# Multiplying the output gate into a copy of the last 128 W_down columns during chunk 3

## The chip, the cores and the metric

The kernel runs on one core of one Trainium2 chip. The metric is the device time in microseconds (us) of one execution. The rounds of the experiments ran on three chips (numbers 5, 3 and 1), each beside runs of the kernel before, and a ratio compares kernels of the same rounds alone. The profile's span is about 1.7 us shorter than the device time of the same run (829.4 against 831.17 us in the first profile), so spans are compared with spans and times with times.

## The reference

A transformer block with adaptive layer-norm: linear attention, then a SwiGLU feed-forward network. S = 2048 tokens, D = 1024, F = 3584, all bf16. Only the end matters for this change:

```
x = A_x
sa, ca, ga, sb, cb, gb = ...            # six rows of D values from the condition c
h = layernorm(x) * (1 + ca) + sa
x = x + ga * attention(h)
h = layernorm(x) * (1 + cb) + sb
x = x + gb * ((silu(h @ w_gate) * (h @ w_up)) @ w_down)
return x
```

`gb` holds one value per output column. Multiplying the product's column n by gb[n] is therefore the same as multiplying column n of `w_down` by gb[n] beforehand, up to rounding to bf16.

## The kernel before

The feed-forward part works in 4 chunks of 512 tokens. In each chunk the kernel first computes 28 tiles of gate and up products (8 + 8 matmuls of 128x512 each), which ScalarE and VectorE turn into the 28 tiles of `AT`. Then 4 token tiles of 128 rows are multiplied with W_down, which lies in SBUF (`WD_A`, `WD_B`) for all chunks. SBUF is the memory in which the kernel keeps its tiles; PSUM (`PS`, in banks) is the one into which its matmuls write. The last part of the program, with the code that the change touches:

```
for ch in range(NCH):                       # NCH = 4
    nxt = ch + 1 if ch + 1 < NCH else None  # None in chunk 3, the last
    for ft in range(NFT):                   # NFT = 28
        gbank, ubank = 2 - (ft % 2) * 2, 3 - (ft % 2) * 2      # PSUM banks alternate
        # ... 8 matmuls into gbank, 8 into ubank ...
        P.act("activation", out=SG[:, ft % 2, :], in_=PS[:, gbank, :], func=ACT.Silu)
        P.dve("tensor_tensor", out=AT[:, ft, :], in0=SG[:, ft % 2, :], in1=PS[:, ubank, :], op=ALU.mult)
        # ... loads; in chunk 0 the gate row GB_B is computed; next chunk's layer norm ...
    for j in range(4):                      # token tiles of the chunk
        st = 4 * ch + j
        bb = 4 + 2 * (st % 2)
        last = st == NST - 1
        # ... if not last: 28 x 2 matmuls into banks bb, bb + 1 ...
        for nh in range(2):                 # halves of the output row
            i = nh
            parts = [(0, 384, bb + 1), (384, 512, 4)] if last and nh == 1 else [(0, 512, bb + nh)]
            for (c0, c1, pb) in parts:
                if last:
                    # ... 28 matmuls over columns c0:c1 of this half ...
                xs = XRES[:, st, nh * 512 + c0:nh * 512 + c1]
                gbs = GB_B[:, nh * 512 + c0:nh * 512 + c1]
                if c0 > 0:
                    P.dve("tensor_tensor", out=UT[:, i, c0:c1], in0=PS[:, pb, c0:c1], in1=gbs, op=ALU.mult)
                else:
                    P.act("activation", out=ATT[:, i, c0:c1], in_=PS[:, pb, c0:c1], func=ACT.Copy)
                    P.dve("tensor_tensor", out=UT[:, i, c0:c1], in0=ATT[:, i, c0:c1], in1=gbs, op=ALU.mult)
                P.dve("tensor_tensor", out=xs, in0=xs, in1=UT[:, i, c0:c1], op=ALU.add)
                out_ops.append(P.dma("out", ov[:, st, nh * 512 + c0:nh * 512 + c1], xs))
```

A helper records every operation, finds from the memory it reads and writes which other engines it has to wait for, and sets the semaphores. In the profile every compute instruction therefore carries that helper's line (L176), and groups are told apart by their tiles.

## Time and profile before

| | before |
|---|---|
| time, median of the first 3 runs | 831.27 us (831.02 to 831.39) |
| span of the profiled run | 829.438 us |
| end of TensorE's last matmul | 826.91 us |
| tail: from there to the end of the span | 2.52 us |

Ends and tails, here and below, are taken from the trace in nanoseconds. The rows of the views print start and duration rounded, so that a sum of them can be off by 0.01 us.

The engines' busy time, the first part of the profile of the kernel before (us, share of the span, instructions):

```profile
PE 824.2 (99%) x4083; PEld 379.2 (46%) x4083; DVE 310.3 (37%) x665; ACT 196.3 (24%) x335; POOL 40.7 (5%) x58
```

The end of the chain of waits (before, from 822 us on; start, duration, what):

```profile
821.94 4.99 PE ps L176 x49
826.93 0.02 issue
826.95 0.30 DVE ut L176
827.25 0.02 issue
827.28 0.23 DVE xres L176
```

The timeline of the same end (before; start, duration, engine, instruction, count, idle time before it and who ended it):

```profile
826.08 0.83 PE L176 MATMUL ps<-wd_b,at 128*128 128x128 bf16 x12
826.38 0.36 DVE L176 TENSOR_TENSOR xres<-xres,ut 128x384 bf16<-128x384 bf16 x1
826.77 1.09 SPq L176 DMA_DIRECT2D out_dram<-xres  x2
826.95 0.29 DVE L176 TENSOR_TENSOR ut<-ps,gb_b 128x128 bf16<-128x128 f32 x1 [0.21 <-PE ps L176]
827.28 0.23 DVE L176 TENSOR_TENSOR xres<-xres,ut 128x128 bf16<-128x128 bf16 x1
```

The last two VectorE instructions are the pair that the change goes for: 0.29 and 0.23 us with a gap between them. The `SPq` row merges the issues of two outputs, of 96 and 32 KB, and its 1.09 us run from the start of the first issue to the end of the second (one issue takes 0.33 us).

VectorE in chunk 3, where the new work is to go (before, timeline of VectorE):

```profile
712.92 0.69 DVE L176 TENSOR_TENSOR at<-sg,ps 128x512 bf16<-128x512 bf16 x1 [2.77 <-PE ps L176]
716.38 0.69 DVE L176 TENSOR_TENSOR at<-sg,ps 128x512 bf16<-128x512 bf16 x1 [2.77 <-PE ps L176]
```

The number in brackets says that VectorE sat idle for 2.77 us of every 3.45 us and that TensorE ended the idle time.

The two last output DMAs (before, DMA view from 826 us on; KB, us from issue to landing):

```profile
out_dram<-xres SPq DMA_DIRECT2D x1, 96.0 KB, 1.6
out_dram<-xres SPq DMA_DIRECT2D x1, 32.0 KB, 1.5
```

### The profile page before, as it was taken

To read this page: it belongs to the slowest core of one execution; us is meant where nothing else is said; L and a number is where in the kernel's file an instruction comes from. 1 tells how busy PE (TensorE), PEld (TensorE's weight loads), DVE (VectorE), ACT (ScalarE), POOL (GpSimd) and SP (SyncE) were. 2 spreads that over 40 slices of the span, in tenths; PEclk is the share of its full clock that TensorE was granted. 3 is DMA by queue.
4 is the path that set the end of the run, shared out by engine and by line. 5 is a ranking of instruction groups with operands and counts; after the bars stand their busy time and mean duration, and the time that the engine had idled before them with its cause. 6 is when DMAs were issued, how large, how long until landed. Compare 5 with 4: busy or idle time off the path is not lost.

```text
span 829.4 us, 10016 instructions
## 1 busy us (share of the span) xinstructions
PE 824.2 (99%) x4083; PEld 379.2 (46%) x4083; DVE 310.3 (37%) x665; ACT 196.3 (24%) x335; POOL 40.7 (5%) x58
## 2 busy tenths in 40 slices
PE   8999999999999999999999999999999999999998
PEld 4544444444444444444444444444444444444444
DVE  5797986666955521111221111122111111111111
ACT  3757641323242111011111101111110111111011
POOL 1010000000130000030000003000000300000000
PEclk9999999999999999999999999999999999999999
DMA  9969655938397985700455571045557004553000
GB/s 324 283 151 230 151 158 172 191 113 304 59 258 226 290 255 154 194 25 13 125 151 152 153 188 31 14 125 153 153 150 193 26 17 123 153 152 89 0 26 26
DMA packets 199246, 119.29 MB, mean 144 GB/s; under 512 B 57880, under 2 KB 182944, under 8 KB 199200
## 3 DMA queue, kind: packets, MB, share of 16 engines
q1 hardware_dynamic: 199184, 118.65, 52.7%
q8 instruction: 32, 0.52, 0.3%
q14 instruction: 14, 0.11, 0.0%
q10 hardware_dynamic: 16, 0.00, 0.0%
HBM read 100.67 MB, written 4.33 MB: 127 GB/s over the span
## 4 chain that ended last, share of the span: by engine, by line
PE 96%; DMA 2%; DVE 1%; SPq 0%; ACT 0%; issue 0%; POOL 0%; ACTq 0%
PE ps L176 96%; DMA z_row<-zr 1%; DMA zb<-z_row 0%; DVE stats L176 0%; DMA xres<-in_A_x_dram 0%; DVE mhl L176 0%; SPq L176 0%; DVE xres L176 0%; DVE pqt L176 0%; POOL rstd L176 0%; DVE g L176 0%; DVE mv L176 0%; ACT gtmp L176 0%; ACT e L176 0%; DVE ve L176 0%
## 5 line engine op out<-in xcount | busy, mean ns | idle before, releaser
L176 PE MATMUL ps<-h2t,gug 128*128 128x512 bf16 x896 | 211.7, 379 | 0.0
L176 PE MATMUL ps<-h2t,guu 128*128 128x512 bf16 x896 | 211.7, 379 | 0.0
L176 DVE TENSOR_TENSOR at<-sg,ps 128x512 bf16<-128x512 bf16 x112 | 77.0, 687 | 284.8 <-PE ps L176 283.2
L176 ACT ACTIVATE sg<-ps 128x512 bf16<-128x512 f32 x112 | 66.9, 597 | 309.7 <-PE ps L176 309.7
L176 PEld LDWEIGHTS ps<-h2t,guu 128*128 128x128 bf16 x896 | 87.7, 98 | 105.7
L176 PEld LDWEIGHTS ps<-h2t,gug 128*128 128x128 bf16 x896 | 87.6, 98 | 105.5
L176 PE MATMUL ps<-wd_a,at 128*128 128x512 bf16 (+2 forms) x528 | 113.5, 373 | 0.0
L176 PE MATMUL ps<-ht,wqk 128*128 128x512 bf16 x512 | 111.8, 379 | 0.1
L176 PE MATMUL ps<-wd_b,at 128*128 128x512 bf16 (+2 forms) x396 | 85.8, 373 | 0.0
L176 PEld LDWEIGHTS ps<-wd_a,at 128*128 128x128 bf16 x528 | 51.1, 98 | 59.8
L176 DVE TENSOR_TENSOR ut<-att,gb_b 128x512 bf16<-128x512 bf16 (+1 forms) x32 | 13.5, 421 | 167.7 <-ACT att L176 167.7
L176 PEld LDWEIGHTS ps<-ht,wqk 128*128 128x128 bf16 x512 | 49.4, 98 | 58.7 <-DVE ht L176 0.4
L176 ACT ACTIVATE att<-ps 128x512 bf16<-128x512 f32 (+1 forms) x32 | 17.4, 591 | 182.1 <-PE ps L176 182.1
L176 PEld LDWEIGHTS ps<-wd_b,at 128*128 128x128 bf16 x396 | 38.3, 98 | 44.7
L176 PE MATMUL ps<-pk,xres 128*128 128x512 bf16 x256 | 56.7, 379 | 0.1
L176 PE MATMUL ps<-mw,pqt 128*128 128x512 bf16 x256 | 56.3, 379 | 0.0
L176 POOL TENSOR_SCALAR h2t<-h2t,modcol 128x512 bf16<-128x512 bf16 x32 | 26.4, 841 | 383.1 <-DMA h2t<-xn 383.1
L176 ACT ACTIVATE e<-ps 128x512 bf16<-128x512 f32 x56 | 33.1, 603 | 31.8 <-PE ps L176 19.6
L176 PEld LDWEIGHTS ps<-mw,pqt 128*128 128x128 bf16 x256 | 24.9, 98 | 30.2 <-DVE xres L176 0.4
L176 PEld LDWEIGHTS ps<-pk,xres 128*128 128x128 bf16 x256 | 24.8, 98 | 30.3 <-DVE g L176 0.6
L176 ACT ACTIVATE junk<-xres 128x1024 bf16<-128x1024 bf16 x24 | 25.4, 1058 | 35.1 <-DVE xres L176 34.9
L176 DVE SCALAR_TENSOR_TENSOR xres<-ps,xres 128x512 bf16<-128x512 f32 x32 | 21.4, 688 | 12.3 <-PE ps L176 11.5
(102 smaller groups left out, 341.1 us busy)
## 6 DMA issues: line engine op xcount, KB each, us to landing
gug<-in_B_w_gate_dram SPq DMA_DIRECT2D x56, 512.0 KB, 4.0
guu<-in_B_w_up_dram SPq DMA_DIRECT2D x56, 512.0 KB, 5.3
xres<-in_A_x_dram SPq DMA_DIRECT2D x20, 256.0 KB, 7.7
rb<-recip_den SPq DMA_DIRECT2D x8, 512.0 KB, 12.1
stgx<-in_w_mod_dram SPq DMA_DIRECT2D x2, 2048.0 KB, 7.9
wd_a<-in_B_w_down_dram SPq DMA_DIRECT2D x4, 1024.0 KB, 7.4
out_dram<-xres SPq DMA_DIRECT2D x31, 128.0 KB, 1.7
xres<-in_A_x_dram SPq DMA_DIRECT2D x3, 1024.0 KB, 14.2
```

The costliest lines, as they stand in the source:

```text
L176: return getattr(e, method)(**kw)
```

## The change

The intent: take one VectorE instruction out of the tail. In chunk 3 VectorE has idle time, so there it multiplies the last 128 columns of W_down by their gate into a separate copy (a copy, because 7 KB per partition are free and the other token tiles keep using the ungated weights). The last 28 matmuls read the copy. What comes out of PSUM is then already gated, and one add of the residual finishes it.

```diff
+        WDG = T("wdg", 144 * KB, [128, NFT, 128], BF16)
...
+                if nxt is None and ft in (8, 12):
+                    f0, f1 = (0, 16) if ft == 8 else (16, NFT)
+                    wt = WD_A if ft == 8 else WD_B
+                    P.dve("tensor_tensor", out=WDG[:, f0:f1, :], in0=wt[:, :, 896:1024],
+                          in1=GB_B[:, 896:1024].unsqueeze(1).to_broadcast([128, f1 - f0, 128]), op=ALU.mult)
...
-                                     rhs=WD(ft)[:, nh * 512 + c0:nh * 512 + c1], start=(ft == 0), stop=(ft == NFT - 1))
+                                     rhs=WDG[:, ft, :] if c0 > 0 else WD(ft)[:, nh * 512 + c0:nh * 512 + c1],
+                                     start=(ft == 0), stop=(ft == NFT - 1))
...
                         if c0 > 0:
-                            P.dve("tensor_tensor", out=UT[:, i, c0:c1], in0=PS[:, pb, c0:c1], in1=gbs, op=ALU.mult)
+                            P.dve("tensor_tensor", out=xs, in0=PS[:, pb, c0:c1], in1=xs, op=ALU.add)
                         else:
                             P.act("activation", out=ATT[:, i, c0:c1], in_=PS[:, pb, c0:c1], func=ACT.Copy)
                             P.dve("tensor_tensor", out=UT[:, i, c0:c1], in0=ATT[:, i, c0:c1], in1=gbs, op=ALU.mult)
-                        P.dve("tensor_tensor", out=xs, in0=xs, in1=UT[:, i, c0:c1], op=ALU.add)
+                            P.dve("tensor_tensor", out=xs, in0=xs, in1=UT[:, i, c0:c1], op=ALU.add)
```

## The prediction

> **What bounds the kernel now.** TensorE. The page's first part has PE busy 824.2 us of a span of 829.4 (99%), DVE 37%; the granted clock is full in every slice. The chain of waits is 96% PE. So only two things move the time: stalls of PE, and the tail after its last matmul.
>
> The tail, from the timeline: the last matmul ends at 826.91. DVE `ut<-ps,gb_b` (128x128, PSUM source) starts at 826.95 and takes 0.29; `xres<-xres,ut` starts at 827.28 and takes 0.23 (end 827.51); the last output DMA (32 KB) is issued at 827.53; it lands about 1.5 us later (DMA view), and the span ends at 829.44. So 2.53 us of tail, 0.56 of it the two VectorE instructions with their gap.
>
> **What the change removes.** The pair becomes one add that reads PSUM and xres, with the shape and operand kinds of the present `ut<-ps,gb_b`: 0.29 us, from 826.95 to 827.24. Removed from the critical path: 0.23 plus the gap of 0.03 to 0.04, so 0.27 us.
>
> **What it adds.** Two VectorE multiplies in chunk 3 (2048 and 1536 elements per partition). An all-SBUF bf16 tensor_tensor took 1.215 us at 2048 elements (`pqt<-pqt,rb`) and 0.42 at 512 (`ut<-att,gb_b`); by their slope the estimates are 1.22 and 0.95 us. [...] Both fit: in chunk 3 DVE idles 2.77 us between consecutive 0.69 us `at<-sg,ps` instructions, and their banks alternate, which gives further slack. Off the critical path: 0 us. PE does the same 28 matmuls of 128 columns; only the moving operand's address differs. The copy lies in space that holds nothing live then, and PE already waits for later VectorE work (the last AT tile), so no new wait. GpSimd has nothing to do in chunk 3.
>
> **What may eat the gain.** The last DMA is issued 0.27 us earlier, at about 827.26, while the preceding 96 KB output (issued 826.77, for 0.33) is moving. In the DMA view its packets run from about 827.57 to 828.06 and the last one's from about 828.27 to 828.57. Moved 0.27 earlier they would start at about 828.00: overlap of 0.06 us at most. I expect 0.2 to 0.27 us to survive. [...] the trace agrees that the time is mostly not data movement (0.3 us of 1.5), and the change does not touch it.
>
> **Prediction.** 831.27 - 0.26 = 831.0 us, range 830.6 to 831.4 (the three runs of before spread 0.37 us, more than the effect). Faster by over 2%: 0.003; within 2%: 0.994; slower by over 2%: 0.003.
>
> **What would show it.** Right: after PE's last matmul one DVE instruction of about 0.29 us, the last output issue about 0.35 us after PE's end instead of 0.62, landing about 1.5 us later; two new DVE instructions of 1.2 and 0.95 us in chunk 3 with PE's idle unchanged; tail about 2.25 us. Wrong: a longer add; a landing of 1.7 us or more (gain lost to contention with the 96 KB transfer); a PE gap behind the multiplies; multiplies over 3.5 us.
>
> **What would make it wrong.** A strided, broadcast multiply far slower than estimated and stalling PE, or landings at the end that hide the gain. Neither reaches 2%.

For the multiplies' 1.22 and 0.95 us the slope between the two measured instructions stays as the ground; that the stride and the broadcast would cost nothing was the assumption, not shown before the run. The 0.3 us of 1.5 is what the trace of before gives for the last output's data packets.

## The result, and the profile after

| | before | after |
|---|---|---|
| time, median of 6 runs each | 831.26 us (831.02 to 832.30) | 831.10 us (830.85 to 831.27) |
| span of the profiled run | 829.438 us | 829.344 us |
| end of TensorE's last matmul | 826.91 us | 827.07 us |
| tail | 2.52 us | 2.27 us |

The ratio of after to before is 0.9997, 95% interval 0.9984 to 1.001: the same. A ratio is the mean time of one kernel's fast runs over that of the other's of the same rounds, so it is not quite the ratio of the medians.

The end of the chain of waits (after, from 822 us on):

```profile
821.94 5.15 PE ps L176 x50
827.09 0.02 issue
827.11 0.29 DVE xres L176
```

The timeline of the end (after):

```profile
825.35 1.73 PE L176 MATMUL ps<-wdg,at 128*128 128x128 bf16 x28
...
826.54 0.36 DVE L176 TENSOR_TENSOR xres<-xres,ut 128x384 bf16<-128x384 bf16 x1
826.93 0.83 SPq L176 DMA_DIRECT2D out_dram<-xres  x2
827.11 0.29 DVE L176 TENSOR_TENSOR xres<-ps,xres 128x128 bf16<-128x128 f32 x1 [0.21 <-PE ps L176]
```

The pair has become one instruction of 0.29 us. The two issues now end 0.83 us after the first one starts instead of 1.09 us: the last output leaves 0.26 us sooner after the one before it.

The two multiplies in chunk 3 (after, timeline of VectorE):

```profile
713.08 0.69 DVE L176 TENSOR_TENSOR at<-sg,ps 128x512 bf16<-128x512 bf16 x1 [2.77 <-PE ps L176]
713.69 1.22 DVE L176 TENSOR_TENSOR wdg<-wd_a,gb_b 128x2048 bf16<-128x2048 bf16 x1
716.54 0.69 DVE L176 TENSOR_TENSOR at<-sg,ps 128x512 bf16<-128x512 bf16 x1 [1.63 <-PE ps L176]
...
727.50 0.95 DVE L176 TENSOR_TENSOR wdg<-wd_b,gb_b 128x1536 bf16<-128x1536 bf16 x1
730.35 0.69 DVE L176 TENSOR_TENSOR at<-sg,ps 128x512 bf16<-128x512 bf16 x1 [1.90 <-PE ps L176]
```

They only eat into the idle time in front of the next `AT` tile: 2.77 us became 1.63 and 1.90. The `AT` tiles themselves keep their pace.

The last two outputs (after, DMA view from 826 us on):

```profile
out_dram<-xres SPq DMA_DIRECT2D x1, 96.0 KB, 1.7
out_dram<-xres SPq DMA_DIRECT2D x1, 32.0 KB, 1.5
```

So the tail is 0.25 us shorter: the last output is issued 0.36 us after TensorE's end instead of 0.62, and lands as long after its issue as before (1.49 against 1.48 us). But TensorE ended 0.16 us later in this trace, and the span shows only the difference, 0.09 us. Does the change delay TensorE? I matched the VectorE instructions of the two traces one by one, in order, and looked at how their start times differ. The difference jumps to 0.41 us at 7.85 us, in the loads and transposes of the start, wanders until 168 us, and from there on its settled value is 0.16 us right up to the end (short excursions of VectorE epilogues come back to it). It is 0.16 us just before the first multiply at 713 us and 0.16 us just after. So nothing is lost where the change is; whether that holds in general is a question for the experiments.

### The profile page after: what moved, and what is told of

Its sections match the earlier page's. It is cut to its first block, busy times and chain, and to the rows that moved or that the text cites. A ratio compares the mean times of both kernels' runs of the same rounds, so it can differ in the third digit from the quotient of the medians.

```text
span 829.3 us, 10017 instructions
## 1 busy us (share of the span) xinstructions
PE 823.3 (99%) x4083; PEld 378.8 (46%) x4083; DVE 312.9 (38%) x666; ACT 196.3 (24%) x335; POOL 40.5 (5%) x58
## 4 chain that ended last, share of the span: by engine, by line
PE 98%; DMA 1%; DVE 0%; ACT 0%; SPq 0%; POOL 0%; issue 0%
PE ps L176 98%; DMA xres<-in_A_x_dram 1%; ACT ht L176 0%; DVE xres L176 0%; SPq L176 0%; POOL rstd L176 0%; DVE stats L176 0%; DVE mv L176 0%; DVE ve L176 0%
## 5 line engine op out<-in xcount | busy, mean ns | idle before, releaser
L176 PE MATMUL ps<-wd_a,at 128*128 128x512 bf16 (+1 forms) x512 | 112.4, 377 | 0.0
L176 PE MATMUL ps<-wd_b,at 128*128 128x512 bf16 (+1 forms) x384 | 85.0, 377 | 0.0
```

The costliest lines, as they stand in the source:

```text
L176: return getattr(e, method)(**kw)
```

## The experiments

Twelve experiments were run. The theory, T: the change takes the quarter of a microsecond out of the tail and does nothing else. The rivals: R1, the gated copy costs TensorE time; R2, the end of the span isn't set by the chain "VectorE, last output"; R3, the slack for VectorE work in chunk 3 is only the idle time that the timeline shows; R4, the last output contends with the 96 KB one before it.

Each experiment left one trace. Its two numbers, TensorE's end and the tail, say more than its times:

| kernel | time, median (lowest to highest) | TensorE's end | tail |
|---|---|---|---|
| before | 831.26 (831.02 to 832.30) | 826.91 | 2.52 |
| before_again | 831.49 (831.35 to 831.66) | 827.23 | 2.52 |
| copy_only | 831.24 (830.85 to 831.50) | 827.23 | 2.53 |
| after | 831.10 (830.85 to 831.27) | 827.07 | 2.27 |
| after_again | 831.34 (830.58 to 831.88) | 827.68 | 2.27 |
| add_only | 830.94 (830.68 to 831.09) | 826.83 | 2.27 |
| mult_x5 | 831.03 (830.92 to 831.19) | 826.96 | 2.28 |
| fold_all | 830.93 (830.78 to 832.08) | 826.93 | 2.26 |
| one_dma | 831.09 (831.02 to 831.46) | 826.83 | 2.50 |
| fold_256 | 831.43 (830.91 to 832.82) | 828.58 | 2.50 |
| tail_x9 | 833.94 (833.76 to 833.99) | 827.05 | 5.12 |
| mult_x8 | 835.57 (833.55 to 836.41) | 829.55 | 2.26 |
| mult_x8_again | 835.55 (one run, state unknown) | 831.57 | 2.26 |
| mult_x10 | 838.49 (838.01 to 839.98) | 835.98 | 2.27 |

### after_again: the changed kernel, unaltered

Expected:

> The changed kernel again, unaltered. Theory T (only the tail after TensorE's last matmul changed): tail from TensorE's end to the span's end about 2.22 us against 2.51 before, time 0.1 to 0.4 us below before. Rival R1 (the gated copy costs TensorE time, so TensorE ends later): the last matmul ends later than in before by 0.1 us or more in this trace too, with the delay entering after 713 us, where the first multiply runs. If instead the delay enters in the first 10 us and has another sign or size than the 0.16 us of the first trace, it is start-up jitter.

Measured: median 831.34 us, ratio 1.0 (0.9987 to 1.0012). The time that T expected was missed: this time the changed kernel wasn't faster at all. The tail was 2.27 us again, 0.26 us shorter than before; the figures in the text above, 2.22 and 2.51, were both a little low. TensorE ended 0.77 us later than in the trace of before, and matching the instructions shows the delay coming in between 7 and 42 us; its settled value is 0.77 us at 168 us and still 0.77 us at 658 us and after. The start-up gives each run another offset, here three times the size of the gain. R1's late entry of a delay isn't there.

### copy_only: the multiplies without their use

```diff
# to the kernel before: the two multiplies into WDG as in the change; nothing reads WDG
```

Expected:

> The two multiplies alone: the gated copy is written and never read, the epilogue is that of before. T: same time as before within 0.15 us, tail 2.51 us as before, multiplies of 1.22 and 0.95 us, TensorE undisturbed after 713 us. R1: slower than before by 0.1 to 0.2 us, and TensorE's offset against before grows after 713 us.

Measured: 831.24 us against 831.26 us, ratio 0.9998 (0.9985 to 1.001). The tail was 2.53 us and the multiplies took 1.218 and 0.952 us. The offset against before was 0.32 us at 168 us and 0.32 us at the end. The copy costs TensorE nothing: R1 falls.

### add_only: the short epilogue without the copy

```diff
# to the changed kernel: no WDG, no multiplies; the last 28 matmuls read the ungated W_down
-                                     rhs=WDG[:, ft, :] if c0 > 0 else WD(ft)[...],
+                                     rhs=WD(ft)[:, nh * 512 + c0:nh * 512 + c1],
```

The last 128 columns are ungated, so the result is wrong on purpose.

Expected:

> The one-add epilogue alone: no copy, the last 128 columns stay ungated, so the result is wrong there on purpose. T: same as the changed kernel, 0.1 to 0.4 us below before, tail about 2.22 us. R1: faster than the changed kernel by 0.1 us or more, because the copy's cost is gone.

Measured: 830.94 us against 831.26 us, ratio 0.9995 (0.9981 to 1.0009), tail 2.27 us. The whole gain is in the epilogue, and it is there without the copy, at the same size. Its time is 0.16 to 0.4 us below that of the changed kernel, which R1 would have liked, but its TensorE simply ended early (826.83 us) by an offset that its trace again brings in at the start (settled at -0.08 us by 168 us and to the end), and copy_only had already shown the copy to be free.

### tail_x9: a longer tail on purpose

```diff
# to the kernel before, the multiply of the last 128 columns out of PSUM
-                            P.dve("tensor_tensor", out=UT[:, i, c0:c1], in0=PS[:, pb, c0:c1], in1=gbs, op=ALU.mult)
+                            for _ in range(9):
+                                P.dve("tensor_tensor", out=UT[:, i, c0:c1], in0=PS[:, pb, c0:c1], in1=gbs, op=ALU.mult)
```

Expected:

> Before, with the last 128-column multiply out of PSUM done nine times instead of once (same result). T: each repetition adds its own time to the span one for one: 8 x (0.29 plus a gap of 0.00 to 0.04) = 2.3 to 2.6 us slower than before, clear of the noise, no change before TensorE's end. Rival R2 (the end of the span is set by something else than the chain VectorE, last DMA, for instance the 96 KB output or a fixed end of program): less than 2 us slower.

Measured: 833.94 us against 831.26 us, ratio 1.0031 (1.0017 to 1.0045). The timeline of its end:

```profile
827.09 2.89 DVE L176 TENSOR_TENSOR ut<-ps,gb_b 128x128 bf16<-128x128 f32 x9 [0.21 <-PE ps L176]
830.01 0.22 DVE L176 TENSOR_TENSOR xres<-xres,ut 128x128 bf16<-128x128 bf16 x1
```

Nine took 2.89 us where one took 0.29, so eight more cost 2.60 us; the tail grew by as much (5.12 against 2.52). The medians differ by 2.68 us, and the rest is within the scatter of the runs. (The traced run's mean clock of 0.998 comes from a fall to half at 829.13 us, when TensorE had no work left, so it cost nothing.) VectorE's time behind the last matmul counts one for one: R2 falls. This is the only kernel of the tail whose effect is clear of the noise in the times themselves.

### before_again: the kernel before against itself

Expected:

> The kernel before, submitted against itself: the noise of this comparison. Both theories: ratio 1.000; tail about 2.53 us in the trace; TensorE's end anywhere between 826.8 and 827.7 us, as in the six traces so far, with the shift entering in the first 45 us. If all traces of the unchanged kernel end TensorE before 827.0 us, a systematic cost of the change in the start-up phase stays possible.

Measured: 831.49 us, against 831.17 us for the runs of the same kernel beside it, ratio 1.0002 (0.9989 to 1.0015). The five runs lie between 831.35 and 831.66 us; eight of the nine beside them between 830.92 and 831.27, one at 832.60. Two medians of one and the same program thus differ by 0.32 us, more than the gain that is looked for. In its trace TensorE ended at 827.23 us, with a settled offset of 0.32 us from 168 us to the end and the tail at 2.52 us. A late TensorE is no sign of the change.

### mult_x5 and mult_x8: how much room VectorE has in chunk 3

```diff
# to the changed kernel, n = 5 or 8
+                    for _ in range(n if ft == 8 else 1):
                         P.dve("tensor_tensor", out=WDG[:, f0:f1, :], in0=wt[:, :, 896:1024], ...
```

Expected of the first:

> The changed kernel with the first multiply written five times in a row (same result): 6.1 us of VectorE work instead of 1.22, more than the 2.77 us of idle up to the next AT tile. T (slack also holds the alternate bank): AT tile 9 ends 6.8 us after AT tile 8, the up matmuls that reuse its bank start 7.9 us after it (estimate: 2.77 plus three groups of 1.73), so TensorE does not wait and the time is that of the changed kernel. Rival R3 (slack is only the 2.77 us of idle): 3.3 us slower.

Measured: 831.03 us, ratio 0.9997 (0.9983 to 1.001), tail 2.27 us. The five multiplies ran from 713.57 us for 6.26 us in a row, `AT` tile 9 was late by about 3.3 us, and TensorE didn't wait at all. R3 falls: with the alternate PSUM bank, 6.26 us of work fitted where the timeline shows 2.77 us of idle time.

Expected of the second:

> The same eight times: 9.75 us of VectorE work. T: AT tile 9 ends 10.4 us after AT tile 8, 2.6 us after its bank is wanted: TensorE waits 2.5 to 2.7 us once, ended by VectorE, and the kernel is 2.5 to 2.7 us slower than the changed kernel. R3: 7 us slower. If there is no wait at all, the slack was underestimated.

Measured: 835.57 us, ratio 1.0054 (1.0039 to 1.007). Its profiled run, of 833.55 us, shows the wait as T expected it, 2.7 us, ended by VectorE (mult_x8, timeline):

```profile
713.29 10.03 DVE L176 TENSOR_TENSOR wdg<-wd_a,gb_b 128x2048 bf16<-128x2048 bf16 x8
...
723.24 1.28 DVE L176 TENSOR_TENSOR at<-sg,ps 128x512 bf16<-128x512 bf16 x2
...
723.98 1.90 PE L176 MATMUL ps<-h2t,guu 128*128 128x512 bf16 x8 [2.70 <-DVE at L176]
```

The eight took 1.25 us each from start to start, where the single one had taken 1.22. But the other three runs took 835.56 to 836.41 us, 2.0 to 2.9 us more than this wait explains, and their mean granted clock was 0.998 where the profiled run had 1.0. That wasn't expected. The next two kernels went after it.

### mult_x10 and mult_x8_again: what a wait of TensorE costs beyond itself

Expected of the tenfold multiply:

> The changed kernel with the first multiply ten times in a row: 12.5 us of VectorE work (1.25 us each as in the eightfold one). T: TensorE waits 2.7 + 2 x 1.25 = 5.2 us once, ended by VectorE. If the wait were all, 5.2 us slower than the changed kernel. The eightfold kernel showed three runs 2 to 2.9 us slower than its 2.6 us wait explains, with a mean granted clock of 0.998; if a wait lowers the granted clock for a stretch after it, all runs here show a clock below 1, the trace shows a stretch after the wait at a lower clock, and the kernel is 7 to 8.5 us slower.

Measured: 838.49 us, ratio 1.0084 (1.0068 to 1.0099), clock 0.996 to 0.998 in all four runs. The timeline of TensorE after the wait (mult_x10; a group of eight matmuls normally takes 1.89 us and starts 1.73 us after the one before it):

```profile
721.03 1.89 PE L176 MATMUL ps<-h2t,gug 128*128 128x512 bf16 x8
728.14 3.59 PE L176 MATMUL ps<-h2t,guu 128*128 128x512 bf16 x8 [5.22 <-DVE at L176]
731.52 2.52 PE L176 MATMUL ps<-h2t,gug 128*128 128x512 bf16 x8
733.88 1.89 PE L176 MATMUL ps<-h2t,guu 128*128 128x512 bf16 x8
```

Two groups ran slowly: from one start to the next they took 3.38 and 2.36 us instead of 1.73, that is 2.28 us more. The group before the wait started 7.11 us ahead of the one after it instead of 1.73, so the wait, printed as 5.22 us of idle, delayed TensorE by 5.38 us; with these 2.28 us that makes 7.66 us. The median is 7.39 us above that of the changed kernel (838.49 - 831.10), the difference being within the scatter of the runs. The stretches of the same trace (mult_x10, busy us of each engine, then the granted clock `PEclk`, DMA share and GB/s):

```profile
721.00:724.00 3.00, 1.92 (x9) 0.69 (x7) 2.90 (x4) 0.00 (x0) 0.00 (x0) 1.00 0.72 182
724.00:728.00 4.00, 0.00 (x0) 0.00 (x0) 3.93 (x5) 0.00 (x0) 0.00 (x0) 0.74 0.00 0
728.00:732.00 4.00, 3.86 (x10) 1.39 (x11) 0.91 (x3) 0.60 (x1) 0.00 (x0) 0.50 0.00 0
732.00:736.00 4.00, 4.00 (x18) 1.72 (x17) 0.65 (x2) 0.60 (x1) 0.00 (x0) 0.90 0.75 213
```

The clock fell to half while TensorE waited, and stayed there from about 725.9 to about 732.8 us (an estimate from these means: 0.74 over 4 us is 2.1 us at half rate, 0.90 is 0.8 us), some 6.9 us.

Expected of the eightfold kernel once more:

> The eightfold kernel once more, for one trace. Of its four runs one kept a mean granted clock of 1.0 and took 833.55 us (that one was traced), three had 0.998 and took 835.6 to 836.4. If the tenfold kernel's account holds (a stretch at half clock after the wait), this run takes either about 833.6 us with clock 1.0 throughout, or about 835.6 us or more with a stretch of 3 to 4 us at clock 0.5 around 722 to 730 us and nothing else changed.

Measured: 835.55 us, clock 0.998: this trace caught the slower kind of run. Timeline of TensorE (mult_x8_again):

```profile
724.31 2.49 PE L176 MATMUL ps<-h2t,guu 128*128 128x512 bf16 x8 [2.70 <-DVE at L176]
726.59 3.03 PE L176 MATMUL ps<-h2t,gug 128*128 128x512 bf16 x8
729.46 1.89 PE L176 MATMUL ps<-h2t,guu 128*128 128x512 bf16 x8
```

And the stretches of the same trace (mult_x8_again, columns as above; the first figure behind the length of the stretch is TensorE's busy time):

```profile
722.07:725.47 3.40, 1.16 (x6) 0.57 (x7) 2.75 (x4) 0.60 (x1) 0.00 (x0) 1.00 0.00 0
725.48:728.89 3.41, 3.41 (x10) 1.24 (x9) 0.69 (x1) 0.00 (x0) 0.00 (x0) 0.50 0.21 53
728.90:732.00 3.10, 3.10 (x16) 1.37 (x14) 0.61 (x2) 0.60 (x1) 0.00 (x0) 1.00 1.02 279
```

The same wait of 2.70 us, but here the clock fell at 725.48 us, 1.2 us after TensorE had already resumed, and stayed at half for 3.41 us. The two groups took 2.28 and 2.87 us from start to start instead of 1.73: 1.69 us more, together. The two traces of this kernel differ by 2.01 us in TensorE's end, and 0.33 us of that is start-up offset (the group before the wait starts at 719.72 against 719.39 us).

The clock records give half rate (0.50) for 3.41 us in this trace and for 6.83 us in mult_x10. In the 3.41 us before the clock fell here, the first row above, TensorE was busy for only 1.16 us. But the trace of mult_x8 has the same wait of 2.70 us, from 721.28 to 723.98 us, and kept its clock (1.00 in every stretch from 712 to 740 us), although in the 3.41 us up to the end of its wait TensorE was busy for just 0.71 us (an estimate from its timeline: 3.41 - 2.70). So one and the same wait came out either way; what decides it was not shown.

A gap of 2.70 us lowered the clock in four runs of five (one of them traced; the other three are known by their mean clock of 0.998 and their times), one of 5.22 us in all four runs of mult_x10 (mean clock 0.996 to 0.998, one of them traced).

None of this touches the changed kernel, whose multiplies stay within the slack. It is the price of overdoing it.

### one_dma: the last two outputs as one

```diff
# to the changed kernel
-                        out_ops.append(P.dma("out", ov[:, st, nh * 512 + c0:nh * 512 + c1], xs))
+                        if last and nh == 1:
+                            if c0 > 0:
+                                out_ops.append(P.dma("out", ov[:, st, 512:1024], XRES[:, st, 512:1024]))
+                        else:
+                            out_ops.append(P.dma("out", ov[:, st, nh * 512 + c0:nh * 512 + c1], xs))
```

Expected:

> The changed kernel with the last two outputs (96 and 32 KB) issued as one of 128 KB after the last add: no transfer to run into, but four times as many bytes behind the last add. T: landing 1.7 to 2.0 us instead of 1.5 and the tail 0.2 to 0.5 us longer than 2.26 us. Rival R4 (the landing is a fixed cost whatever the bytes, and the 96 KB transfer contends with the last one): tail equal to or below 2.26 us.

Measured: tail 2.50 us, 0.23 us longer than the changed kernel's, and in the DMA view (one_dma):

```profile
out_dram<-xres SPq DMA_DIRECT2D x1, 128.0 KB, 1.7
```

The landing took 1.7 us instead of 1.5. Four times the bytes cost 0.23 us, and R4's tail of 2.26 us or less didn't come. The time, 831.09 us (0.9998, 0.9986 to 1.0011), shows none of it: TensorE happened to end early, at 826.83 us.

### fold_all and fold_256: gating all of W_down in chunk 3

```diff
# fold_all, to the kernel before
+                if nxt is None and ft < NFT:
+                    P.dve("tensor_tensor", out=WD(ft), in0=WD(ft), in1=GB_B[:], op=ALU.mult)
...
-                        if c0 > 0:
-                            P.dve("tensor_tensor", out=UT[:, i, c0:c1], in0=PS[:, pb, c0:c1], in1=gbs, op=ALU.mult)
+                        if nxt is None:
+                            P.dve("tensor_tensor", out=xs, in0=PS[:, pb, c0:c1], in1=xs, op=ALU.add)
# ... the other branch as before, for chunks 0 to 2 ...
# fold_256, besides
-                    parts = [(0, 384, bb + 1), (384, 512, 4)] if last and nh == 1 else [(0, 512, bb + nh)]
+                    parts = [(0, 256, bb + 1), (256, 512, 4)] if last and nh == 1 else [(0, 512, bb + nh)]
```

Expected of fold_all:

> Before, with the gate multiplied in place into every W_down tile during chunk 3 (28 multiplies of 1024 elements, estimate 0.68 us each from the same shape on W_o, into 2.77 us of idle), so that every epilogue of chunk 3, the 384-column one too, is one add out of PSUM. The 96 KB output then leaves about 0.6 us earlier, clear of the last one. T (no contention in the changed kernel): tail as in the changed kernel, 2.22 to 2.28 us, no TensorE wait. R4 (the 96 KB transfer still costs the last one something): tail at or below 2.15 us, last landing under 1.45 us.

Measured: 830.93 us, ratio 0.9998 (0.9985 to 1.001), tail 2.26 us, no wait of TensorE; the multiplies took 0.684 us each. Its timeline:

```profile
825.41 0.56 DVE L176 TENSOR_TENSOR xres<-ps,xres 128x384 bf16<-128x384 f32 x1 [3.86 <-PE ps L176]
...
826.97 0.29 DVE L176 TENSOR_TENSOR xres<-ps,xres 128x128 bf16<-128x128 f32 x1 [1.00 <-PE ps L176]
```

The 384 columns were done 1.00 us before the last add could start, so their output was issued 1.30 us ahead of the last one instead of 0.50; and the last one still needed as long as in the changed kernel, 1.49 us to landing and the same tail within 0.01 us. R4 falls: in the changed kernel the data packets of the two transfers nearly touch (827.76 to 828.20 and 828.26 to 828.52 us in its trace) but don't overlap, and cost each other nothing that the tail shows.

Expected of fold_256:

> The same with the last half row split 256/256 instead of 384/128. T: the last add takes 0.42 us instead of 0.29 (estimate from 0.29 at 128 and 0.69 at 512 columns), the last output is 64 KB and lands 0.05 to 0.15 us later, so the tail is 2.4 to 2.55 us; TensorE's last stage gets 0.1 to 0.2 us shorter, because a 128-column matmul takes 62 ns from start to start and a 384-column one 162 (their sum is 8 ns more than a 512-column one, 216). Sum against the changed kernel: -0.05 to +0.25 us, not to be seen in the times.

Measured: 831.43 us, ratio 1.0003 (0.9991 to 1.0016), tail 2.50 us as T had it (the last add took 0.42 us). The other half of what was expected was wrong: TensorE's last stage wasn't any shorter. From the start of the first matmuls of the split half row to the end of the last it took 6.28 us, against 6.27 us in fold_all (822.30 to 828.58, and 820.66 to 826.93). The error was in the 62 ns for a 128-column matmul: that was 1.73 us divided by 28, and the 1.73 us include the last matmul's run to its end. From start to start, 16 of them took 0.89 us in fold_all (825.21 to 826.10), 56 ns each; with 162.5 ns at 384 columns the sum is 218 ns, and two of 256 columns (1.75 us for 16) also take 219. TensorE's late end in this trace (828.58 us) came from the start: its offset against before settled at 1.67 us by 168 us and stayed.

No version beat the changed kernel: fold_all has the same tail with more work, the other two have a longer one.

## Why the prediction was right

The prediction was 831.0 us with a range of 830.6 to 831.4; the medians were 831.10 and, in the second set, 831.34 us, both the same as before within 2%. That the time fell into the range proves little: the median of the kernel before, 831.26 us, lies in it too. What confirms the prediction is what it said of the traces.

- **TensorE bounds the kernel, and only the tail is left to win.** Right. tail_x9 shows that time behind the last matmul counts one for one (2.60 us added, 2.60 us longer), mult_x5 that more VectorE time in chunk 3 counts nothing as long as it fits into the slack.
- **0.27 us removed.** Right to 0.02 us: 2.52 us of tail in both traces of the kernel before, and 2.53 in copy_only; 2.27 us in both traces of the changed kernel, and in add_only. That is 0.25 us less; predicted was a tail of about 2.25 us. The last output was issued 0.36 us after TensorE's end (predicted: 0.35) instead of 0.62.
- **The new add takes 0.29 us.** Right. It swaps one operand for another of the same kind and is as long as the multiply that it replaces (0.29 us).
- **The multiplies take 1.22 and 0.95 us, despite the stride and the broadcast.** Right: 1.218 and 0.951 us. In the trace of the kernel before, a `tensor_tensor` on 2048 bf16 elements from SBUF with both operands contiguous (`pqt<-pqt,rb`) took 1.215 us; with one operand in runs of 128 elements, 2048 bytes apart, and the other broadcast (outer stride zero) it took 1.218 us here.
- **They are off the critical path.** Right, by copy_only. The "further slack" is a measured quantity now: 6.26 us of extra work in one step cost nothing, 10.03 us made TensorE wait 2.70.
- **The 96 KB output might eat 0 to 0.07 us of the gain.** It ate nothing that shows: tails of 2.27 and 2.26 us with the earlier output issued 0.50 us ahead of the last one (826.93 and 827.43) and 1.30 us ahead (fold_all). The feared overlap of 0.06 us came from packet times read off a coarse view; the data packets stay 0.06 us apart. The trace of the kernel before splits the 1.48 us of the last one (32 KB) into 0.83 us from issue to the first data packet, 0.26 us of data packets and 0.39 us from the last packet to the landing, and 96 KB more cost 0.23 us of tail in one_dma. The estimate of the gain did not rest on the split, only on a landing that stays as long (1.48 us before, 1.49 after).
- **What can be seen in the times.** Little, as the prediction said. Put together, the 25 runs of kernels with the short tail (after, after_again, add_only, mult_x5, fold_all) average 831.11 us, the 43 with the long one (before in all timed rounds, before_again, copy_only) 831.33 us: -0.23 us, with a standard error of 0.09 from their spread of 0.35 us each. This grouping was chosen afterwards, from what the traces showed. The changed kernel's 11 runs alone, against the 38 of the kernel before, give -0.16 us with a standard error of 0.12. Both agree with 0.25 us, and neither would have shown it alone.

What stays open is the cause of the start-up offset. It moved TensorE's end by 0.9 us between traces of kernels that should end it at the same moment (826.83 to 827.68 us), and by 1.7 us in one more (fold_256). The traces show when it enters (most of it in the first 45 us, among loads, transposes and layer norm, the rest by 168 us) and that it then stays, but no run here varied the start. One candidate does not explain it: the moment at which the clock records first show full rate. It is 7.99 us in the trace of before and earlier in before_again and after_again (5.41 and 5.59 us), whose TensorE yet ended 0.32 and 0.77 us later.

## What to carry to other kernels

In this kernel, where one engine is busy 99% of the span, the instructions between its last one and the last output counted one for one (2.60 us of them cost 2.60 us in tail_x9), and moving their work into another engine's idle time was free as long as it fitted into the slack, which was set by when the buffer was wanted again and not by the idle time before the next instruction (6.26 us fitted in mult_x5, where 2.77 us were idle). Measure such a gain as the length of the tail in the trace, not as a difference of times: here two medians of one and the same program differed by 0.32 us, more than the gain of 0.25 us, and in the traces the offset of TensorE's end came in within the first 168 us. And don't let background work overrun its slack: a wait of 2.7 us of TensorE cost 1.7 us more through the clock in the run that was traced with it, one of 5.22 us cost 2.3 us more.
